# Attention and a gated feed-forward layer in one kernel: where v is loaded, and where the turned q and k are taken apart

## The chip, the core and the metric

The kernel runs on one core of a Trainium2 chip. The metric is device time in microseconds (us) for one execution. The core's engines run side by side, each on a queue of its own in a fixed order: TensorE (PE) for matmuls, VectorE (DVE), ScalarE (ACT), GpSimd (POOL), and SyncE (SP), which here only issues DMAs. ScalarE and GpSimd can issue DMAs too; such an issue stands in their queue between their other instructions. An engine that needs another's result waits at that instruction, and all behind it on the same engine waits with it.

## The reference

Eight batches of eight heads, 576 positions, head size 64. The scores get a bias from a running sum of `s`, a causal mask, a softmax, and are multiplied by v. The heads' outputs, laid side by side, are the 4608 x 512 input of a feed-forward layer with a hard-swish between its two products.

```python
scores = scale * np.matmul(q, k.transpose(0, 1, 3, 2))
cum = np.cumsum(np.maximum(s, 0.0), axis=-1)
bias = -(cum[:, :, :, None] - cum[:, :, None, :])
scores = np.where(causal, -1000000000.0, scores + np.minimum(bias, 0.0))
attn = softmax(scores)
x = np.matmul(attn, v)             # then to (4608, 512)
h = x @ w_in                       # 512 -> 2048
out = (h * np.clip(h + 3.0, 0.0, 6.0) / 6.0) @ w_out
```

## The kernel before

The 64 heads are worked in 32 pairs (two heads of one batch). Everything for TensorE is float16. For each pair q and k must stand with the head dimension on the partitions: `qT` and `kT`, two parts of `qkT`, in `NS` = 3 slots by pair number modulo 3. Rows 64 to 67 of a slot hold the bias terms (`load_aug`).

How q and k get there depends on the pair. Pairs 0 to 3 are cast and turned by TensorE (`cast_first`, `turn_first`, L825 to L837), pairs 4 to 9 as well (`transpose_group`, L301, L316). From pair `PTD` = 10 on, GpSimd casts them into `xb` (`cast_beside`, L282), SyncE issues a transposing DMA into `turned` (`transpose_dma`, L285), q in partitions 0 to 63 and k in 64 to 127, and VectorE copies both into the slot: `apart`, L293 for q and L294 for k.

v is loaded by `load_v` in three DMAs: one for each head's first 512 rows (L218) and one for the last 64 rows of both (L222). GpSimd casts it to `v_h` (`cast_v`, L298). v has three slots too.

`scores_bank` makes a head's scores in four pieces, each in one bank of PSUM (L350). ScalarE takes the exponential into `Pm` (L357), GpSimd zeroes what is above the diagonal (L362). The banks come from a ring of three (tag `S`), so a piece waits until the exponential three pieces earlier is done. `attend` multiplies with v (L447); VectorE divides by the row sums (L463, L464); `x_transpose` brings the result into `xT`, from pair 8 on by a transposing DMA on SyncE (L481).

The feed-forward layer goes in nine blocks of 512 rows. `m1` makes 128 of the 2048 columns (L526); ScalarE applies a relu with bias 3 (`trl`, L536), VectorE the gate (`gT`, L537), which frees the bank. `m2` is the second product (L569); its result goes through `osb` (L584) to the output (L586).

The order on each engine is the order of the calls in the program. Three stretches follow each other:

- a loop over the first eight heads (pairs 0 to 3). In it `cast_v(p)` is called at the first head of pair p. At pair 1 the two main loads of v of pair 3 are issued by GpSimd, its small one by SyncE. The weights are issued by GpSimd in and after this loop. A small DMA, the fence (L936), makes SyncE wait for `w_out`; the loads of later pairs stand behind it.
- pairs 4 to 8 in `second_pair`, among products of block 0.
- pairs 9 to 31 in `att_tasks`, which gives a list of small tasks with costs; `weave` deals them among the products of a block, in proportion to cost. For pair p the list has, in this order: `attend` of the earlier pair's second head, `x_transpose(p - 1)`, `loads` (q, k and v of pair p + 3), the four pieces of the first head (`s0`), those of the second (`s1`) with `apart(p + 1)` ahead of the third, `casts` (`cast_v(p + 1)`, `load_aug(p + 3)`, `cast_beside(p + 2)`, `transpose_dma(p + 2)`). `attend` of the first head follows.

Waits are on semaphores. The hardware DMAs share eight completion semaphores in turn, and a DMA first waits for the one before it on its semaphore.

Of the kernel before, what the change touches and what calls it, by code (L numbers as in the profile page):

```python
# [16 lines left out]
def kernel(  # L17
# [10 lines left out]
    nc = tc.nc  # L28
# [7 lines left out]
    W2 = 2 * SEQ  # L36
# [10 lines left out]
    PXD = 8  # L47
    NS = 3
# [37 lines left out]
    qT, kT = qkT[:, :, 0:W2], qkT[:, :, W2:SLOTW]  # L86
# [4 lines left out]
    turned = cpool.tile([128, 2, W2], F16, tag="c_turned")  # L91
# [106 lines left out]
    def qk_tile(p):  # L198
        qk_f[p] = work.tile([128, NTR, 2, D], F32, tag="qkf", bufs=3, name=f"qkf{p}")

    def load_part(p, i, t0, t1, eng):
        b, h0 = (2 * p) // H, (2 * p) % H
        rows = (q, k)[i][b, h0:h0 + 2].rearrange("h s d -> (h s) d")
        eng.dma_start(  # L204
            out=qk_f[p][:, t0:t1, i, :],
            in_=rows.rearrange("(t p) d -> p t d", p=128)[:, t0:t1, :],
        )

    def load_qk(p, eng):
        qk_tile(p)  # L210
        for i in range(2):
            load_part(p, i, 0, NTR, eng)

    def load_v(p, eng, main=None):
        b, h0 = (2 * p) // H, (2 * p) % H
        sl = p % NS
        for hh in range(2):
            (main or eng).dma_start(  # L218
                out=v_f[:, sl, hh, 0:4, :],
                in_=v[b, h0 + hh, 0:512].rearrange("(t p) d -> p t d", p=128),  # L220
            )
        eng.dma_start(  # L222
            out=v_f[0:64, sl, :, 4, :],
            in_=v[b, h0:h0 + 2, 512:SEQ].rearrange("h p d -> p h d"),
        )

    def load_aug(p, eng):
        sl = p % NS
        part = [h1 > 2 * p for _, h1 in PARTS].index(True)
        c0 = (2 * p - PARTS[part][0]) * SEQ  # L230
        eng.dma_start(
            out=qkT[64:68, sl, 0:2 * W2].rearrange("r (i c) -> r i c", i=2),
            in_=aug_dram[part][:, :, c0:c0 + W2].rearrange("i r c -> r i c"),
        )

    def cast_qk(p):
        t = work.tile([128, NTR, 2, D], F16, tag="qkh", bufs=2)
        src = qk_f.pop(p)
        for t0, t1 in ((0, 5), (5, 9)):
            nc.gpsimd.tensor_copy(out=t[:, t0:t1], in_=src[:, t0:t1])  # L240
        qk_h[p] = t
# [39 lines left out]
    def cast_beside(p):  # L281
        nc.gpsimd.tensor_copy(out=xb[:, p % 2], in_=qk_f.pop(p))  # L282

    def transpose_dma(p):
        nc.sync.dma_start(  # L285
            out=turned[:, p % 2, :].rearrange("p (t c) -> p t c", c=128),
            in_=xb[:, p % 2].rearrange("p t i d -> p (t i d)"),
            transpose=True,
        )

    def apart(p):
        sl = p % NS
        nc.vector.tensor_copy(out=qT[0:64, sl, :], in_=turned[0:64, p % 2, :])  # L293
        nc.vector.tensor_copy(out=kT[0:64, sl, 0:W2], in_=turned[64:128, p % 2, :])  # L294

    def cast_v(p):
        sl = p % NS
        nc.gpsimd.tensor_copy(out=v_h[:, sl, :, :, 0:D], in_=v_f[:, sl])  # L298
# [6 lines left out]
    def transpose_group(p, g):  # L305
        t0, t1 = ((0, 5), (5, 9))[g]
        n = (t1 - t0) * 128
        pT = f16(PS[:, 3, :], n)
        src = qk_h[p]
        for t in range(t0, t1):  # L310
            c = (t - t0) * 128
            transpose_tile(pT[:, c:c + 128], src[:, t, :, :], t == t0, t == t1 - 1)
        sl = p % NS
        c0 = t0 * 128
        for dst, r0 in ((qT, 0), (kT, 64)):
            nc.vector.tensor_copy(out=dst[0:64, sl, c0:c0 + n], in_=pT[r0:r0 + 64, 0:n])  # L316
        if g == 1:
            qk_h.pop(p)
# [152 lines left out]
    def by_dma(p):  # L471


        return PXD <= p < NP - 1

    def x_transpose(p):
        b, hp = p // (H // 2), p % (H // 2)
        xs = x_tiles.pop(p)
        if by_dma(p):

            nc.sync.dma_start(  # L481
                out=xT[:, hp, b * SEQ:b * SEQ + 640].rearrange("p (t c) -> p t c", c=128),
                in_=xs.rearrange("p t h d -> p (t h d)"),
                transpose=True,
            )
            return
        pX = f16(PS[:, 4 if p + 1 < FIRST else 2, :], 640) if p < FIRST else f16(bank("S"), 640)
        for qt in range(5):
            nc.tensor.matmul(
                out=pX[:, qt * 128:(qt + 1) * 128],  # L490
                lhsT=xs[:, qt, :, :],
                rhs=ident,
                is_transpose=True,
                start=(qt == 0),
                stop=(qt == 4),
            )
        nc.vector.tensor_copy(out=xT[:, hp, b * SEQ:(b + 1) * SEQ], in_=pX[:, 0:SEQ])
# [121 lines left out]
    def store_aug(part):  # L619
        h0, h1 = PARTS[part]  # L620
        nc.sync.dma_start(
            out=aug_dram[part].rearrange("i r (h t) -> h (i r) t", t=SEQ),
            in_=aug[h0:h1].rearrange("h i r t -> h (i r) t"),
        )

    def load_pair(p):
        load_qk(p, nc.sync)
        load_v(p, nc.sync)

    def scores(hd):  # L630
        return [(lambda bi=bi: scores_bank(hd, bi), 400) for bi in range(4)]
# [4 lines left out]
    def att_tasks(p):  # L636


        more = p + 1 < NP

        def loads():
            if p + 3 < NP:
                load_pair(p + 3)
            if p < PTD - 1:
                cast_qk(p + 1)

        def casts():
            if more:
                cast_v(p + 1)
            if p + 3 < NP:  # L650
                load_aug(p + 3, nc.sync)
            if p - PXD in (1, 2):
                store_aug(p - PXD + 2)
            if PTD <= p + 2 < NP:
                cast_beside(p + 2)
                transpose_dma(p + 2)

        tr = [[], []]
        if p + 1 < min(NP, PTD):
            tr = [[(lambda: transpose_group(p + 1, 0), 640)],  # L660
                  [(lambda: transpose_group(p + 1, 1), 512)]]
        late = [(lambda: attend(2 * p - 1), 600 if PTD <= p < PTD + 3 else 1200)]
        back = []
        if p > FIRST:
            back = [(lambda: x_transpose(p - 1), 0 if by_dma(p - 1) else 640)]
        a = [(loads, 0)]
        if p <= PXD:
            a += scores(2 * p) + tr[0] + late
            a += scores(2 * p + 1) + [(casts, 0)] + tr[1] + back
        else:  # L670
            s0, s1 = scores(2 * p), scores(2 * p + 1)
            a = late + (back + a if by_dma(p - 1) else a + s0[:2] + back)
            a += (s0 if by_dma(p - 1) else s0[2:]) + tr[0]
            if PTD <= p + 1 < NP:
                s1.insert(2, (lambda: apart(p + 1), 0))
            a += s1 + [(casts, 0)] + tr[1]
        return a, [(lambda: attend(2 * p), 1800 if PTD <= p + 1 < PTD + 3 else 1200)]

# [46 lines left out]
    def values(hd):  # L725
        return [
            [(lambda: attend(hd, range(0, 3)), 480)], [(lambda: attend(hd, range(3, 5)), 720)]
        ]

    att_of = [[]]  # L730
    for p in range(PXD, NP):
        a, c = att_tasks(p)
# [143 lines left out]
    def cast_pair(p):  # L876
        for i in range(2):
            cast_first(p, i, 0, NTR, G.tensor_copy)
            if p == 3 and i == 0:
                load_w_in(0)  # L880
        qk_f.pop(p)
# [3 lines left out]
    for hd in range(2 * FIRST):  # L885
        p, odd = hd // 2, hd % 2
        scores_half(hd, 0)
        if hd == 0:
            turn_first(0, 0, 5, 9, 6, V.tensor_copy)
            turn_first(0, 1, 5, 9, 5, V.tensor_copy)  # L890
        if not odd:
            if p == 0:
                cast_pair(1)
            if p == 2:
                load_w_in(1)
            cast_v(p)
            if p == 1:
                load_v(3, nc.sync, nc.gpsimd)
            if p + 1 < FIRST:
                turn_first(p + 1, 0, 0, 9, 4, V.tensor_copy)  # L900
            if p == 2:
                load_w_in(2)
            if p == 0:
                load_qk(3, nc.sync)
                nc.sync.dma_start(out=s_sb, in_=s.rearrange("b h t -> (b h) t"))
                load_v(2, nc.sync)
        elif p + 1 < FIRST:
            turn_first(p + 1, 1, 0, 9, 4, V.tensor_copy)
            if p + 2 < FIRST:
                cast_pair(p + 2)  # L910
        scores_half(hd, 1)
        if hd > 0:
            attend(hd - 1)
        if odd and p > 0:
            x_transpose(p - 1)
# [106 lines left out]
```

## Time and profile before

| what | value |
|---|---|
| median of 3 runs | 351.65 us (351.3 to 353.86) |
| profiled execution, and its span | 353.66 us, 351.9 us |
| granted TensorE clock | 1.000 |
| TensorE busy | 342.1 us, 97% of the span |
| VectorE, ScalarE, GpSimd busy | 58%, 59%, 42% |
| loads of v from SyncE, 128 KB each (L218) | 62, median 708 ns |
| loads of v from SyncE, 32 KB each (L222) | 32, median 627 ns |
| loads of v from GpSimd (L218) | 2, median 856 ns |

A line of the waits reads: engine, line, the engine and line it waited for, us in total, times, the longest. A line of the timeline reads: start, duration, engine, line, operation, what is written from what, and in brackets the idle time just before and what ended it. "SPq" is SyncE's issuing of a DMA: its duration is the issue, not the transfer. TensorE's matmuls overlap, so that its busy time is no measure of peak rate; gaps between its instructions are what counts here.

### The profile page before, as it was taken

To read this page: it belongs to the slowest core of one execution; us is meant where nothing else is said; L and a number is where in the kernel's file an instruction comes from. 1 tells how busy PE (TensorE), PEld (TensorE's weight loads), DVE (VectorE), ACT (ScalarE), POOL (GpSimd) and SP (SyncE) were. 2 spreads that over 40 slices of the span, in tenths; PEclk is the share of its full clock that TensorE was granted. 3 is DMA by queue.
4 is the path that set the end of the run, shared out by engine and by line. 5 is a ranking of instruction groups with operands and counts; after the bars stand their busy time and mean duration, and the time that the engine had idled before them with its cause. 6 is when DMAs were issued, how large, how long until landed. Compare 5 with 4: busy or idle time off the path is not lost.

```text
span 351.9 us, 7619 instructions
## 1 busy us (share of the span) xinstructions
PE 342.1 (97%) x2797; PEld 199.8 (57%) x2797; DVE 205.2 (58%) x375; ACT 208.7 (59%) x393; POOL 149.0 (42%) x322
## 2 busy tenths in 40 slices
PE   7899999999999899999999999999999999999996
PEld 3775457655555555555555555555555545444444
DVE  6559568887555783566546654756365635644531
ACT  4767747787655685677467755775577615534410
POOL 4685657744655356545435444454444200000000
PEclk9999999999999999999999999999999999999999
DMA  9999899999999888989898789788923110010012
GB/s 181 226 167 215 195 225 213 233 225 183 172 204 228 186 172 191 214 188 140 198 195 176 157 168 220 149 177 173 219 43 82 50 60 32 16 45 30 30 60 91
DMA packets 160271, 53.91 MB, mean 153 GB/s; under 512 B 152394, under 2 KB 154122, under 8 KB 160234
## 3 DMA queue, kind: packets, MB, share of 16 engines
q1 hardware_dynamic: 157178, 48.68, 63.9%
q0 software_dynamic: 2256, 4.46, 6.8%
q8 instruction: 22, 0.36, 0.4%
q10 hardware_dynamic: 800, 0.30, 0.3%
q14 instruction: 15, 0.12, 0.1%
HBM read 37.40 MB, written 9.95 MB: 135 GB/s over the span
## 4 chain that ended last, share of the span: by engine, by line
PE 76%; DMA 11%; DVE 4%; SPq 4%; POOL 2%; issue 1%; ACT 1%; POOLq 0%; ACTq 0%
PE PS L569 31%; PE PS L526 28%; PE PS L350 10%; PE PS L447 6%; DMA w_out_sb<-in_moe_w_out_dram 5%; DMA turned<-xb 3%; SPq L204 1%; SPq L218 1%; DMA qkf<-in_k_dram 1%; DVE gT L537 1%; DMA v_f<-in_v_dram 1%; DVE qkT L316 1%; PE PS L595 1%; DVE qkT L294 1%; PE PS L301 1%
## 5 line engine op out<-in xcount | busy, mean ns | idle before, releaser
L526 PE MATMUL PS<-xT,w_in 128*128 128x512 f16 x576 | 142.8, 380 | 1.8 <-DVE gT L537 1.8
L536 ACT ACTIVATE trl<-PS,bias 128x512 f32<-128x512 f32 x144 | 98.5, 693 | 74.3 <-PE PS L526 73.7
L537 DVE SCALAR_TENSOR_TENSOR gT<-trl,PS 128x512 f16<-128x512 f32 x144 | 97.4, 686 | 76.4 <-ACT trl L536 75.9
L569 PE MATMUL PS<-w_out_sb,gT 128*128 128x512 f16 x560 | 138.3, 379 | 0.0
L357 ACT ACTIVATE Pm<-PS 128x384 f16<-128x384 f32 x224 | 101.5, 508 | 41.6 <-PE PS L350 40.6
L362 POOL TENSOR_SCALAR_AFFINE_SELECT Pm<-Pm 128x64 f16<-128x64 f16 (+2 forms) x214 | 70.0, 330 | 111.3 <-ACT Pm L357 102.5
L526 PEld LDWEIGHTS <-w_in 128*128 128x128 f16 x576 | 60.3, 114 | 46.1 <-issue 2.4
L569 PEld LDWEIGHTS <-gT 128*128 128x128 f16 x560 | 51.1, 98 | 49.2 <-issue 0.3
L350 PE MATMUL PS<-qkT 128*128 128x256 f16 x392 | 61.5, 261 | 1.0 <-DVE qkT L294 0.6
L350 PEld LDWEIGHTS <-qkT 128*128 128x128 f16 x392 | 36.3, 98 | 30.3 <-DVE qkT L316 1.4
L447 PEld LDWEIGHTS <-Pm 128*128 128x128 f16 x960 | 38.0, 97 | 11.2 <-POOL Pm L362 0.3
L447 PE MATMUL PS<-v_h,Pm 128*128 128x65 f16 x960 | 41.1, 193 | 0.2 <-POOL Pm L362 0.2
L584 DVE TENSOR_SCALAR osb<-PS 128x512 f32<-128x512 f32 x34 | 23.4, 687 | 26.1 <-PE PS L569 26.1
L464 DVE TENSOR_TENSOR xs<-PS,r 128x640 f16<-128x640 f32 (+1 forms) x37 | 27.2, 735 | 1.3
L282 POOL CAST xb<-qkf 128x1152 f16<-128x1152 f32 x22 | 26.1, 1188 | 1.0 <-DMA qkf<-in_k_dram 1.0
L298 POOL CAST v_h<-v_f 128x640 f16<-128x640 f32 x32 | 23.7, 740 | 3.1 <-DMA v_f<-in_v_dram 3.0
L293 DVE COPY qkT<-turned 64x1152 f16<-64x1152 f16 x22 | 11.6, 527 | 11.5 <-DMA turned<-xb 11.5
L431 ACT ACTIVATE Pm<-PS 128x896 f16<-128x896 f32 (+1 forms) x16 | 13.1, 836 | 5.6 <-PE PS L425 5.5
L294 DVE COPY qkT<-turned 64x1152 f16<-64x1152 f16 x22 | 13.4, 611 | 0.3
L463 DVE RECIPROCAL r<-PS 128x10 f32<-128x10 f32 (+1 forms) x37 | 7.7, 209 | 6.1 <-PE PS L447 5.8
L316 DVE COPY qkT<-PS 64x640 f16<-64x640 f16 (+1 forms) x20 | 9.1, 454 | 2.3 <-PE PS L301 1.9
L425 PE MATMUL PS<-qkT 68*128 68x64 f16 (+4 forms) x48 | 9.1, 277 | 0.5 <-DVE qkT L837 0.4
(89 smaller groups left out, 115.4 us busy)
## 6 DMA issues: line engine op xcount, KB each, us to landing
out_dram<-osb SPq DMA_DIRECT2D x35, 256.0 KB, 2.6
qkf<-in_q_dram SPq DMA_DIRECT2D x31, 288.0 KB, 3.6
qkf<-in_k_dram SPq DMA_DIRECT2D x31, 288.0 KB, 4.1
v_f<-in_v_dram SPq DMA_DIRECT2D x62, 128.0 KB, 3.7
w_out_sb<-in_moe_w_out_dram POOLq DMA_DIRECT2D x4, 512.0 KB, 16.6
v_f<-in_v_dram SPq DMA_DIRECT2D x32, 32.0 KB, 2.6
w_in<-in_moe_w_in_dram POOLq DMA_DIRECT2D x2, 512.0 KB, 6.9
w_in<-in_moe_w_in_dram POOLq DMA_DIRECT2D x1, 1024.0 KB, 11.9
```

What stands on the lines that cost most here:

```text
L282: nc.gpsimd.tensor_copy(out=xb[:, p % 2], in_=qk_f.pop(p))
L298: nc.gpsimd.tensor_copy(out=v_h[:, sl, :, :, 0:D], in_=v_f[:, sl])
L350: nc.tensor.matmul(out=S[:, c:c + hi - lo], lhsT=kT[:, sl, off + 128 * kt:off + 128 * (kt + 1)], rhs=qT[:, sl, off + lo:off + hi], start=( ...
L357: nc.scalar.activation(out=P[:, p0:p0 + n], in_=S[:, 0:n], func=AF.Exp, scale=0.125, bias=0.0)
L362: nc.gpsimd.affine_select(out=view, in_=view, pattern=pattern, compare_op=ALU.is_ge, fill=0.0, base=0, channel_multiplier=-1,)
L447: nc.tensor.matmul(out=O[:, hh, qt * VW:qt * VW + D + 1], lhsT=P[:, c:c + 128], rhs=v_h[:, sl, hh, kt, 0:D + 1], start=(qt == 0), stop=(qt ...
L464: nc.vector.tensor_tensor(out=x_tiles[p].rearrange("p t h d -> p h t d")[:, heads], in0=Ov[:, :, :, 0:D], in1=r[:, 0:n].to_broadcast([128, ...
L526: nc.tensor.matmul(out=ph, lhsT=w_in_t[f // 4][:, kc, f % 4, :], rhs=xT[:, kc, n * 512:(n + 1) * 512], start=(kc == 0), stop=(kc == KC - 1),)
L536: nc.scalar.activation(out=trl, in_=ph, func=AF.Relu, bias=bias3[:, 0:1], scale=1.0)
L537: nc.vector.scalar_tensor_tensor(out=gT2[:, n % 2, f, :], in0=trl, scalar=6.0, in1=ph, op0=ALU.min, op1=ALU.mult)
L569: nc.tensor.matmul(out=po, lhsT=gT2[:, n % 2, f, t4 * 128:(t4 + 1) * 128], rhs=w_out_sb[:, f, :], start=(f == 0), stop=(f == NF - 1),)
L584: nc.vector.tensor_scalar_mul(out=osb, in0=pouts[n, t4], scalar1=1.0 / 6.0)
```

## The change

It has three parts.

1. In the loop over the first pairs, `load_v(3, ...)` is called ahead of `cast_v(1)`, where it was called behind it. On GpSimd the two issues now stand ahead of the cast; SyncE's part stands where it stood.
2. `apart` copies one of q and k. For pairs 10 to 31 the copy of q stays where it was, ahead of the third piece of the second head; the copy of k comes behind the fourth piece.
3. In pairs 11, 12 and 13 (`V_BY_ACT`) v of pairs 14, 15 and 16 is no longer issued by SyncE behind q and k, but by ScalarE behind the fourth piece of the first head: three DMAs each time.

```diff
-    def apart(p):
-        sl = p % NS
-        nc.vector.tensor_copy(out=qT[0:64, sl, :], in_=turned[0:64, p % 2, :])
-        nc.vector.tensor_copy(out=kT[0:64, sl, 0:W2], in_=turned[64:128, p % 2, :])
+    def apart(p, i):
+        nc.vector.tensor_copy(
+            out=(qT, kT)[i][0:64, p % NS, 0:W2], in_=turned[64 * i:64 * i + 64, p % 2, :]
+        )
...
             if p + 3 < NP:
-                load_pair(p + 3)
+                load_qk(p + 3, nc.sync)
+                if p not in V_BY_ACT:
+                    load_v(p + 3, nc.sync)
...
             a += (s0 if by_dma(p - 1) else s0[2:]) + tr[0]
+            if p in V_BY_ACT:
+                a.append((lambda: load_v(p + 3, nc.scalar), 0))
             if PTD <= p + 1 < NP:
-                s1.insert(2, (lambda: apart(p + 1), 0))
+                s1.insert(2, (lambda: apart(p + 1, 0), 0))
+                s1.append((lambda: apart(p + 1, 1), 0))
             a += s1 + [(casts, 0)] + tr[1]
...
+    V_BY_ACT = range(PXD + 3, PXD + 6)
     att_of = [[]]
...
                 load_w_in(1)
-            cast_v(p)
             if p == 1:
                 load_v(3, nc.sync, nc.gpsimd)
+            cast_v(p)
```

## The prediction

> **What bounds the kernel now.** I read the page's busy shares first, then who waited for whom, then stretches of the timeline around each wait of TensorE.
>
> ```profile
> PE 342.1 (97%) x2797; PEld 199.8 (57%) x2797; DVE 205.2 (58%) x375; ACT 208.7 (59%) x393; POOL 149.0 (42%) x322
> PE PS L526 <- DVE gT L537: 1.8, 2, 1.3
> PE PS L831 <- POOL gT L825: 1.3, 2, 0.9
> PE PS L350 <- DVE qkT L294: 0.6, 1, 0.6
> DVE qkT L293 <- DMA turned<-xb: 11.5, 9, 4.0
> ```
>
> TensorE is busy 97%, and its list of waits is short: less than 10 us idle in 352, and from 118 us to 345 us it is never idle. A change can win only these idles, and loses whenever it makes a new one, because a late TensorE catches up nowhere. Three idles touch the edited lines. The first is at 17 us:
>
> ```profile
> 14.15 0.72 POOL L298 CAST v_h<-v_f 128x640 f16<-128x640 f32 x1 [1.59 <-DMA v_f<-in_v_dram]
> 14.82 1.70 POOL L218 DMA_DIRECT2D v_f<-in_v_dram  x2
> 16.50 0.69 POOL L825 CAST gT<-qkf 128x576 f16<-128x576 f32 x1
> 17.25 0.69 PE L831 MATMUL PS<-idtri,gT 128*68 128x128 f16 x9 [0.90 <-POOL gT L825]
> ```
>
> GpSimd waits 1.59 us for v of pair 1, casts it, and only then spends 1.70 us issuing v of pair 3; the cast that TensorE needs stands behind. The others lie where pairs 12 and 14 are prepared:
>
> ```profile
> 94.43 1.65 SPq L285 DMA_TRANSPOSE turned<-xb  x1
> 98.65 0.98 DVE L293 COPY qkT<-turned 64x1152 f16<-64x1152 f16 x1 [3.99 <-DMA turned<-xb]
> 99.65 1.30 DVE L294 COPY qkT<-turned 64x1152 f16<-64x1152 f16 x1
> 101.01 0.34 PE L350 MATMUL PS<-qkT 128*128 128x256 f16 x2 [0.61 <-DVE qkT L294]
> 114.89 0.55 DVE L293 COPY qkT<-turned 64x1152 f16<-64x1152 f16 x1 [0.78 <-DMA turned<-xb]
> 115.45 1.31 DVE L294 COPY qkT<-turned 64x1152 f16<-64x1152 f16 x1
> 116.79 1.88 DVE L537 SCALAR_TENSOR_TENSOR gT<-trl,PS 128x512 f16<-128x512 f32 x3
> 117.53 1.89 PE L526 MATMUL PS<-xT,w_in 128*128 128x512 f16 x8 [1.26 <-DVE gT L537]
> 99.76 1.71 SPq L218 DMA_DIRECT2D v_f<-in_v_dram  x2
> 101.51 0.63 SPq L222 DMA_DIRECT2D v_f<-in_v_dram  x1
> ```
>
> The two copies wait for the transposed load, which is late because SyncE issues without a gap from 40.05 us (the fence behind w_out) to 127 us; v takes 1.71 + 0.63 = 2.34 us of each pair's issuing. In time of issue TensorE loses about 0.75 us at 101 us, 1.4 us at 117.5 us, and a third idle at 82.4 us (0.6 us, gT behind the two copies of pair 10).
>
> **What the Trainium skill says.** Perfetto Trace Analysis, "What 'DMA-bound' means": an issuing sequencer whose track is solid DMA slices is itself a bound. The trace agrees for SyncE, 40 to 127 us. The same page, "DMA Instruction — HWDGE (DVE, Sync)": the sequencer is held for the lock on a shared descriptor generator and while it works, and is free only at the reported end. The trace agrees for SyncE (slices 0.04 to 0.1 us apart); it has no such load amid ScalarE's exponentials. DMA: Bandwidth & Descriptors, "Issuing engines are not separate DMA queues": another issuer saves the sequencer's time, not transfer time; no line of before tests it. SBUF — State Buffer, "SBUF: two separate sides": VectorE's fast modes and GpSimd exclude each other for a whole instruction. The trace agrees: the k copy takes 0.46 us, and 1.30 us where it meets GpSimd's 1.38 us cast at 99.27 us.
>
> **The change part by part.**
>
> *v of pair 3 ahead of the cast.* The two issues keep their price (1.70 us) but fall into GpSimd's 1.59 us of waiting, which starts at 12.56: done at 14.26, the cast until 14.98, then q of pair 3, whose load I place at about 15.2 (issued at 10.93; the two before it took some 4 us). That cast ends near 15.9, before TensorE asks at 16.24. TensorE gains 1.0 us. The gain lasts only if SyncE's chain moves too, since TensorE meets it at 101 us. That chain begins when w_out lands (40.04 us); the weights stream at a DMA share above 1 from 20 us, after a dip to 0.51 at 18 to 19 us, and their first load is issued about 1.0 us earlier. So **−1.0 us**, between −1.2 and 0 (0 if the early bytes only delay v of pair 1 or w_out).
>
> *Copies apart.* 22 more places in the order, no new work. Pair 9: one gT product moves ahead of the 0.46 us k copy, **−0.46 us**. In pairs 10 to 12 the two copies stay neighbours on VectorE. From pair 14 on the k copy comes up to about 1 us later; what hides it is the two attends and the products between the last score of a pair and the next pair's first (144.28 us against a k copy done at 141.33). It now falls nearer to GpSimd's casts and may take 1.3 instead of 0.46 us; gT waits 76 us for ScalarE in all, so that is room: 0, with +1.5 us as the other bound.
>
> *v of pairs 14 to 16 by ScalarE.* Nine issues leave SyncE (3 x 2.34 us). In the built program every hardware DMA first waits for the one eight places back on the shared completion semaphores, whichever engine issues it: transposes of x on SyncE now stand behind a v that ScalarE has to issue (pair 10's behind v of pair 14: issued about 96.1, landing near 99, so it goes 2 us later than its 97.20). The slot's earlier cast is long done. So SyncE gains little for pair 13's load, and two to three us for pair 14's, which GpSimd's cast then sets.
> On ScalarE the three issues hold back four exponentials of the second head. The score ring has three banks, so the second head's fourth score waits for its first exponential. The price on ScalarE is unknown: 1.4 us with the shortest v issue of SyncE (0.379 twice, 0.6), 2.34 us at SyncE's usual, 3 us if each also waits for SyncE's turn. I take 2.0 us, 0.4 of it under the exponential ahead, which is still running: 1.6 us. Then:
> - pair 11: the first exponential ends at about 96.5, the fourth score starts at 97.5: slack 0.95, stall 0.65 us. It meets the 0.75 us idle at 101 us and the 0.46 us of pair 9, 1.2 us together: **−0.55 us for both**. The k copy can follow it, since GpSimd's cast is late as well and no longer meets it.
> - pair 12: slack 0.25 us, and a 0.16 us gap ahead of pair 13 goes: 1.6 − 0.25 − 0.16 = **+1.2 us**.
> - pair 13: behind a relu of 0.69 us that hides part of it, no slack: +1.3 us. The 1.4 us idle at 117.5 goes, since copy and gT are no longer late against TensorE; the k copy now sits between two gT products and costs about 0.4 us: **+0.3 us**.
>
> Sum: −1.0 − 0.55 + 1.2 + 0.3 = −0.05 us. To this I add 0.4 us for transfers that now run beside pair 12's transposed load (4.19 us already) and for longer k copies: **+0.35 us**. The profiled execution took 353.66 us (span 351.9 and 1.8 around it), so it would take 354.0. It stands 2.0 us above the median of the runs shown, 351.65; the forecast for the median is **352.0 us**.
>
> **The rivals.**
> 1. ScalarE's issues are nearly hidden (0.8 us left). For it: 0.47 us for its only early load, and an empty ring of its own. Pair 11 costs nothing and wins 1.2, pair 12 costs 0.4, pair 13 wins 0.9: −1.0 − 1.2 + 0.4 − 0.9 = −2.7, 349.0 us. Against it: v takes SyncE 1.5 to 1.9 us for two even at 212 to 251 us, where the transfers are less dense.
> 2. Slower: ScalarE's issues stand in SyncE's way and are stood in the way of, at pairs 11 to 13, 1 us each, 3 us a pair. Pair 11 +0.45, pair 12 +2.2, pair 13 +1.3, and nothing won at the start: +3.95, 355.6 us. It passes +1% (3.5 us) from about 0.95 us an issue, if the start wins nothing. For it: SyncE is solid there. Against it: 0.71 us is the median of a v issue.
> 3. The early order gives nothing (SyncE's chain, held by bandwidth, takes it back at 101 us) and the rest is as forecast: 353.0 us.
>
> **How the numbers follow.** Forecast 0.55 (350.8 to 353.4), rival 1 0.20, rival 2 0.13, rival 3 0.12. Leaving out the lower half of rival 1 and the upper of rival 2 gives 349.8 to 354.9. About 1% (3.5 us) is what a measurement of this kernel tells from no change: faster by more needs nearly all idle gone, 0.03; slower by more is rival 2's upper part and what I overlook, 0.11; within, 0.86.
>
> **What would show it.** Right: no wait of L831 for GpSimd at 16 us, w_out landing near 39 us, new idles of TensorE at L350 <- ScalarE L357 in pairs 12 and 13 of 1 to 1.5 us, no idle for gT after pair 13, ScalarE's v issues of 0.5 to 0.8 us each. Wrong: those issues below 0.4 us or above 1 us, a wait of ScalarE for a DMA, or new idles after 125 us from late k copies.

## The result, and the profile after

| | before | after |
|---|---|---|
| median of 6 runs | 352.33 us (351.30 to 353.86) | 355.76 us (355.26 to 357.67) |
| ratio, with 95% interval | | 1.0092 (1.0066 to 1.0118) |
| profiled execution, and its span | 353.66 us, 351.9 us | 355.26 us, 353.5 us |

The kernel became slower by 0.9%, some 3.2 us. The forecast was no change, 352.0 us in a range to 354.9; it was wrong. The two profiled executions differ by only 1.6 us: that of before stands 1.3 us above its median, that of after 0.5 us below. The traces show where time goes; how much it is in the mean, the ratios of many runs tell.

TensorE's share of after, and who waited for whom:

```profile
PE 342.6 (97%) x2797; PEld 200.2 (57%) x2797; DVE 207.7 (59%) x375; ACT 209.1 (59%) x393; POOL 149.1 (42%) x322
PE PS L350 <- ACT Pm L357: 3.6, 4, 1.5
PE PS L526 <- DVE gT L537: 0.4, 1, 0.4
PE PS L837 <- POOL gT L831: 0.4, 1, 0.4
DVE qkT L292 <- DMA turned<-xb: 12.7, 5, 4.7
```

TensorE does the same work. Its waits for gT at L526 went from 1.8 to 0.4 us. Those for GpSimd's casts of q and k went from 1.3 to 0.4 us: the one at 17 us (0.9 us) is gone, an earlier one of 0.4 us stays. The wait for a k copy is gone too. One new wait outweighs them: scores that wait for ScalarE's exponential.

The start of after, timeline of GpSimd:

```profile
12.38 1.70 POOL L218 DMA_DIRECT2D v_f<-in_v_dram  x2
14.06 0.74 POOL L298 CAST v_h<-v_f 128x640 f16<-128x640 f32 x1
15.37 0.67 POOL L831 CAST gT<-qkf 128x576 f16<-128x576 f32 x1 [0.56 <-DMA qkf<-in_q_dram]
18.84 0.72 POOL L298 CAST v_h<-v_f 128x640 f16<-128x640 f32 x1 [0.76 <-DMA v_f<-in_v_dram]
```

This is as forecast: the issues lie in the former wait, and the cast of q of pair 3 starts at 15.37 instead of 16.50. Further back GpSimd waits 0.76 us for v of pair 2, where it had not waited.

Pair 11 of after, ScalarE ("ACTq" is its issuing of a DMA), and TensorE at the fourth scores of the second heads of pairs 11, 12 and 13:

```profile
93.97 0.49 ACT L357 ACTIVATE Pm<-PS 128x384 f16<-128x384 f32 x1 [0.27 <-PE PS L350]
94.20 0.38 ACTq L218 DMA_DIRECT2D v_f<-in_v_dram  x1
94.35 0.43 ACT L357 ACTIVATE Pm<-PS 128x320 f16<-128x320 f32 x1
94.68 1.19 ACTq L218 DMA_DIRECT2D v_f<-in_v_dram  x1
95.96 0.69 ACTq L222 DMA_DIRECT2D v_f<-in_v_dram  x1
96.75 1.69 ACT L357 ACTIVATE Pm<-PS 128x384 f16<-128x384 f32 x4 [1.97 <-PE PS L569]
97.30 0.30 PE L350 MATMUL PS<-qkT 128*128 128x320 f16 x1 [1.01 <-ACT Pm L357]
105.50 0.30 PE L350 MATMUL PS<-qkT 128*128 128x320 f16 x1 [1.45 <-ACT Pm L357]
114.39 0.30 PE L350 MATMUL PS<-qkT 128*128 128x320 f16 x1 [0.96 <-ACT Pm L357]
```

The first exponential of the second head waits behind the issues, and the score that needs its bank waits with it. Where TensorE stands at the first score of each pair:

| first score of pair | before | after | difference |
|---|---|---|---|
| 11 | 93.64 | 92.29 | −1.35 |
| 12 | 101.01 | 100.07 | −0.94 |
| 13 | 108.64 | 109.43 | +0.79 |
| 14 | 119.25 | 120.35 | +1.10 |
| 16 | 135.95 | 137.54 | +1.59 |

TensorE of after is ahead by 1.35 us when it comes to pair 11, loses 2.45 us until pair 14 and 0.5 us until pair 16. From there the difference stays.

### The profile page after: what moved, and what is told of

The parts are those of the page before. It is cut to its first block, busy times and chain, and to the rows that moved or that the text cites. A ratio compares the mean times of both kernels' runs of the same rounds, so it can differ in the third digit from the quotient of the medians.

```text
span 353.5 us, 7655 instructions
## 1 busy us (share of the span) xinstructions
PE 342.6 (97%) x2797; PEld 200.2 (57%) x2797; DVE 207.7 (59%) x375; ACT 209.1 (59%) x393; POOL 149.1 (42%) x322
## 4 chain that ended last, share of the span: by engine, by line
PE 82%; SPq 4%; ACT 3%; DVE 3%; DMA 3%; issue 2%; POOL 2%; ACTq 1%; POOLq 0%
PE PS L569 32%; PE PS L526 31%; PE PS L350 9%; PE PS L447 7%; DMA turned<-xb 2%; ACT Pm L357 2%; SPq L204 1%; SPq L218 1%; DVE gT L537 1%; DVE qkT L292 1%; DMA v_f<-in_v_dram 1%; PE PS L595 1%; ACT trl L536 1%; POOL Pm L362 1%; PE PS L301 1%
## 5 line engine op out<-in xcount | busy, mean ns | idle before, releaser
L526 PE MATMUL PS<-xT,w_in 128*128 128x512 f16 x576 | 142.7, 379 | 0.5 <-DVE gT L537 0.4
L357 ACT ACTIVATE Pm<-PS 128x384 f16<-128x384 f32 x224 | 101.6, 509 | 45.1 <-PE PS L350 40.7
L362 POOL TENSOR_SCALAR_AFFINE_SELECT Pm<-Pm 128x64 f16<-128x64 f16 (+2 forms) x214 | 69.2, 326 | 116.3 <-ACT Pm L357 107.3
L526 PEld LDWEIGHTS <-w_in 128*128 128x128 f16 x576 | 60.2, 113 | 45.7 <-issue 1.9
L350 PE MATMUL PS<-qkT 128*128 128x256 f16 x392 | 61.8, 261 | 4.0 <-ACT Pm L357 3.6
L350 PEld LDWEIGHTS <-qkT 128*128 128x128 f16 x392 | 36.3, 98 | 29.7 <-DVE qkT L316 1.4
L292 DVE COPY qkT<-turned 64x1152 f16<-64x1152 f16 x44 | 28.6, 650 | 13.3 <-DMA turned<-xb 12.7
```

The costliest lines, as they stand in the source:

```text
L292: nc.vector.tensor_copy(out=(qT, kT)[i][0:64, p % NS, 0:W2], in_=turned[64 * i:64 * i + 64, p % 2, :])
L350: nc.tensor.matmul(out=S[:, c:c + hi - lo], lhsT=kT[:, sl, off + 128 * kt:off + 128 * (kt + 1)], rhs=qT[:, sl, off + lo:off + hi], start=( ...
L357: nc.scalar.activation(out=P[:, p0:p0 + n], in_=S[:, 0:n], func=AF.Exp, scale=0.125, bias=0.0)
L362: nc.gpsimd.affine_select(out=view, in_=view, pattern=pattern, compare_op=ALU.is_ge, fill=0.0, base=0, channel_multiplier=-1,)
L526: nc.tensor.matmul(out=ph, lhsT=w_in_t[f // 4][:, kc, f % 4, :], rhs=xT[:, kc, n * 512:(n + 1) * 512], start=(kc == 0), stop=(kc == KC - 1),)
```

## The experiments

Two theories at first. A: ScalarE's issues hold the second head's exponentials, and that is the whole loss. B: the k copies behind the fourth piece make it. Later C: SyncE's waits for transfers that ScalarE issues.

### Each part alone

Only the loads by ScalarE (SyncE no longer issues them, as in the change):

```diff
+            if p in V_BY_ACT:
+                a.append((lambda: load_v(p + 3, nc.scalar), 0))
```

> Only the loads of v of pairs 14 to 16 go to ScalarE; order of v of pair 3 and the copies as before. Theory A (ScalarE's issues hold the second head's exponentials, and that is the whole loss): idles of TensorE at L350 behind ScalarE of 1.0, 1.5 and 1.0 us in pairs 11 to 13, and +3 to +4 us against before, as much as the whole change or a little more. Theory B (the k copies behind the fourth piece make the loss): the loads alone cost under 1 us, since the idles of before at 101 and 117 us take them up.

Measured: 1.0072 (1.0045 to 1.0099), 2.5 us, with 1.6 to 3.5 us in the interval. B, which gave this part under 1 us, falls by this ratio; the part alone is most of the loss. For A it is a little less than expected.

Its profiled execution is a poor sample. From 84 to 90 us the granted TensorE clock was 0.50 to 0.85, and by 92 us TensorE was 3.4 us behind the trace of before, although ScalarE's first load is issued only at 98.97 us. From 92 us on the clock is 1.00, and the three idles are there:

```profile
101.41 0.30 PE L350 MATMUL PS<-qkT 128*128 128x320 f16 x1 [0.36 <-ACT Pm L357]
109.34 0.30 PE L350 MATMUL PS<-qkT 128*128 128x320 f16 x1 [1.17 <-ACT Pm L357]
118.07 0.30 PE L350 MATMUL PS<-qkT 128*128 128x320 f16 x1 [1.11 <-ACT Pm L357]
```

But from there to the end it loses only 0.75 us more against the trace of before, because the idles that before had at 101 and 117.5 us are gone, as B had it. The ratio speaks for more; why this one trace shows less stays open.

Only the copies apart (`apart` takes one of the two, as in the change):

```diff
-                s1.insert(2, (lambda: apart(p + 1), 0))
+                s1.insert(2, (lambda: apart(p + 1, 0), 0))
+                s1.append((lambda: apart(p + 1, 1), 0))
```

> Only the copies of q and k apart. Theory A: within 0.5 us of before, no idle of TensorE for a copy. Theory B: +2 us or more, with idles at L526 or L569 behind gT where a k copy stands between two products of the gate, one or two of them after 125 us.

Measured: 1.0013 (0.9998 to 1.0028). Set matmul by matmul against before, each counted from its first, TensorE wins 0.72 us at 78 to 84 us and gives 0.64 us back between 122 and 135 us. The give-back is in all eight profiles with the copies apart (0.48 to 0.64 us) and in none of the four others that have them together (0.00 us). Its place, with the k copy of pair 15 in before (first line) and then VectorE and the product behind it in after:

```profile
125.00 0.46 DVE L294 COPY qkT<-turned 64x1152 f16<-64x1152 f16 x1
128.04 1.10 DVE L292 COPY qkT<-turned 64x1152 f16<-64x1152 f16 x1
129.17 0.69 DVE L537 SCALAR_TENSOR_TENSOR gT<-trl,PS 128x512 f16<-128x512 f32 x1
130.77 1.87 DVE L537 SCALAR_TENSOR_TENSOR gT<-trl,PS 128x512 f16<-128x512 f32 x3
131.50 1.02 PE L569 MATMUL PS<-w_out_sb,gT 128*128 128x512 f16 x4 [0.18 <-DVE gT L537]
```

In after the k copy runs beside GpSimd's cast (127.68 to 128.83 us), takes 1.10 us for 0.46, and the gate's products behind it are late for the first product of `m2`. It is not the only one: of the 44 copies of q and k, 38 to 42 took under 0.6 us in the five profiles with the copies together, 25 to 31 in the eight with them apart.

Only v of pair 3 early:

```diff
-            cast_v(p)
             if p == 1:
                 load_v(3, nc.sync, nc.gpsimd)
+            cast_v(p)
```

> Only v of pair 3 asked for ahead of the cast. Both theories: the wait of L831 for GpSimd at 17 us is gone, w_out lands 2 to 3 us earlier. If TensorE keeps that, -1.0 us; if it is given back at the transposed loads of pairs 12 and 14, within 0.3 us of before.

Measured: 0.9999 (0.9984 to 1.0013), so between −0.6 and +0.5 us. The wait at 17 us is gone, and w_out landed at 38.95 us, 1.1 us earlier, less than expected. But in this execution 0.69 us is won by 16.5 us and only 0.15 us is left at 20.5 us. The first line is before, the others are this run:

```profile
19.18 0.77 POOL L298 CAST v_h<-v_f 128x640 f16<-128x640 f32 x1
19.31 0.72 POOL L298 CAST v_h<-v_f 128x640 f16<-128x640 f32 x1 [0.98 <-DMA v_f<-in_v_dram]
20.08 0.58 PE L447 MATMUL PS<-v_h,Pm 128*128 128x65 f16 x14 [0.48 <-POOL v_h L298]
```

GpSimd comes to the cast of v of pair 2 earlier than in before, but v of pair 2 is not there earlier. So GpSimd waits 0.98 us for it, and TensorE 0.48 us for GpSimd. All nine profiles with the early order show such a wait of GpSimd, of 0.7 to 1.0 us. The cast begins at 18.7 to 19.7 us in them, and at 19.1 to 19.7 us in the four with the old order; that the early bytes made v of pair 2 later is not shown.

How much TensorE keeps differs from one execution to the next. At 40 us, matmul by matmul against before, it stands at −0.8 to +0.3 us in the nine (mean −0.3) and at −0.1 to +0.5 us in the four, before among them (mean +0.1). Nor was the idle at 17 us in each: in the run with only ScalarE's loads, which has the old order, GpSimd waited 0.53 us for v of pair 1 and not 1.59, and the idle is not there. It then waited 0.89 us for v of pair 2 all the same.

The kernel before, once more:

> The kernel before, looked at once more, since its six runs lie in two groups (351.3 to 351.7 and 353.0 to 353.9) and its profiled run is in the upper. If the groups differ by the idles at 101 and 117 us, a run near 351.5 shows less than 1 us of idle for L294 and gT there, and the gain that the forecast saw in them is mostly not there. If they do not, its trace has both idles (0.6 and 1.3 us) as the first has. Time: 1.000 of before.

Measured: 1.0015 (0.9997 to 1.0033); the profiled execution took 353.75 us. TensorE's waits for gT, and for a copy of k:

```profile
PE PS L526 <- DVE gT L537: 1.9, 2, 1.5
PE PS L350 <- DVE qkT L294: 0.2, 1, 0.2
```

The idle for gT is there, that at 101 us is not. So the idle at 101 us comes and goes from one execution to the next. What an execution of 351.3 us looks like stays open; none was profiled.

### The hold of ScalarE by itself

The changed kernel again, then without these loads:

> The changed kernel once more, beside the others of this call. Ratio to before 1.006 to 1.012, and again three idles of TensorE for ScalarE at L350 in pairs 11 to 13, 3 to 4 us in all.

Measured: 1.0076 (1.0048 to 1.0105), waits at L350 for ScalarE of 3.9 us.

```diff
-            if p in V_BY_ACT:
-                a.append((lambda: load_v(p + 3, nc.scalar), 0))
```

> The changed kernel without any load of v of pairs 14 to 16 (the slots keep older values, so the output of these pairs is not the reference's). ScalarE is not held and SyncE is relieved. Theory A (the hold of ScalarE is the loss): no idle at L350 for ScalarE, 3 to 4.5 us under the changed kernel, so 0.5 to 1 us under before. Theory C (SyncE's waits for transfers of another engine's issue are the loss): about as theory A. If it stays over +0.5% against before, neither holds, and the loss lies in the copies.

Measured: 0.9954 (0.9935 to 0.9972). No score waits for ScalarE beyond 0.2 us. SyncE issues pair 14's transposed load at 106.95 us, against 111.18 in before. So SyncE's relief is worth something, 0.4% against the two other parts without it (0.9996, measured below), and ScalarE's three times three issues take it back three times over. This run lacks the transfers of these v as well as their issues; the run with the same loads behind the second head (0.9947, below) has them and is as fast, so the gain is not that of missing transfers.

ScalarE held without any DMA (`scratch` is a tile for this alone):

```diff
+    def hold():
+        for _ in range(4):
+            nc.scalar.copy(out=scratch, in_=warm)
...
-                a.append((lambda: load_v(p + 3, nc.scalar), 0))
+                a.append((hold, 0))
```

> As the run without loads of v of pairs 14 to 16, but with four copies of 128 x 512 in fp16 on ScalarE where the three issues stood, some 2.0 to 2.3 us of work without any DMA (the output of these pairs is not the reference's). Theory A: as slow as the changed kernel within 1 us, with the same three idles at L350. Theory C: as fast as the run without the loads.

Its lines are numbered one higher: L351 is L350 of before, L358 is L357. ScalarE's copies, and TensorE:

```profile
96.14 2.57 ACT L639 COPY scratch<-warm 128x512 f16<-128x512 f16 x4
104.93 2.56 ACT L639 COPY scratch<-warm 128x512 f16<-128x512 f16 x4
114.76 2.56 ACT L639 COPY scratch<-warm 128x512 f16<-128x512 f16 x4
99.15 0.30 PE L351 MATMUL PS<-qkT 128*128 128x320 f16 x1 [1.40 <-ACT Pm L358]
107.93 0.30 PE L351 MATMUL PS<-qkT 128*128 128x320 f16 x1 [2.02 <-ACT Pm L358]
117.75 0.30 PE L351 MATMUL PS<-qkT 128*128 128x320 f16 x1 [2.21 <-ACT Pm L358]
```

Measured: 1.0141 (1.0111 to 1.0171). The stand-in is longer than meant, 2.56 us, and the three idles grow with it, to 5.6 us. The time was expected within 1 us of the changed kernel and is 2.3 us over. The longer idles make 1.9 us in the traces (scores for ScalarE: 5.8 us for 3.9). But three of the six executions also had a mean clock of 0.994 to 0.995, which none of the changed kernel's six had, and the other three are only 1.2 us over; how the excess divides is not settled. C falls as the explanation: the loss is there without a transfer.

### The same loads in other places

Behind the second head, where ScalarE then has nothing to do for 2.4 us in pair 11 and 3.4 us in pair 12:

```diff
-            if p in V_BY_ACT:
-                a.append((lambda: load_v(p + 3, nc.scalar), 0))
...
+            if p in V_BY_ACT:
+                s1.append((lambda: load_v(p + 3, nc.scalar), 0))
```

> The changed kernel with ScalarE's loads moved behind the fourth piece of the second head, where ScalarE stands idle for about 3 us in pairs 11 and 12; in pair 13 four relus stand behind them. Theory A: no idle at L350 for ScalarE, pairs 11 and 12 cost nothing, pair 13 costs up to 1.5 us at L526 behind gT; in all 0.995 to 1.004 of before. Theory C: still slow, 1.006 or more, since the loads land later still and SyncE waits longer for them.

ScalarE of this kernel in pair 11, and all waits of TensorE between 90 and 136 us:

```profile
97.06 0.44 ACT L357 ACTIVATE Pm<-PS 128x320 f16<-128x320 f32 x1 [0.19 <-PE PS L350]
97.16 1.08 ACTq L218 DMA_DIRECT2D v_f<-in_v_dram  x2
98.34 0.69 ACTq L222 DMA_DIRECT2D v_f<-in_v_dram  x1
99.86 0.49 ACT L357 ACTIVATE Pm<-PS 128x384 f16<-128x384 f32 x1 [2.37 <-PE PS L350]
107.30 0.56 PE L350 MATMUL PS<-qkT 128*128 128x256 f16 x4 [0.24 <-DVE qkT L292]
116.20 1.02 PE L526 MATMUL PS<-xT,w_in 128*128 128x512 f16 x4 [0.40 <-DVE gT L537]
128.21 1.02 PE L569 MATMUL PS<-w_out_sb,gT 128*128 128x512 f16 x4 [0.18 <-DVE gT L537]
```

Measured: 0.9947 (0.9930 to 0.9964), 351.76 us: under both kernels, with the same loads by the same engine. The nine issues last nearly as long as in after (4.9 us for 5.3 us), and the next exponential, the first of pair 12, waits for its scores, not for them. This settles A against C.

One exponential later than in after:

```diff
-            if p in V_BY_ACT:
-                a.append((lambda: load_v(p + 3, nc.scalar), 0))
...
+            if p in V_BY_ACT:
+                s1.insert(1, (lambda: load_v(p + 3, nc.scalar), 0))
```

> The changed kernel with ScalarE's loads one exponential later: behind the first piece of the second head in place of behind the last of the first. Theory A as the ring of three banks has it: the fourth piece of the second head needs only the first piece's exponential, which now stands ahead of the loads, so the idles at L350 for ScalarE are gone, 0.995 to 1.001 of before. If any hold of ScalarE among the scores costs its length, the time stays at 1.006 or more.

Measured: 1.0052 (1.0036 to 1.0067). The idles at L350 for ScalarE are gone, so the ring of three banks is how the hold reached the scores. But most of the loss is still there, against what was expected. VectorE and TensorE of this kernel:

```profile
99.89 1.86 DVE L292 COPY qkT<-turned 64x1152 f16<-64x1152 f16 x2 [5.45 <-DMA turned<-xb]
117.63 1.27 DVE L292 COPY qkT<-turned 64x1152 f16<-64x1152 f16 x1
101.81 0.34 PE L350 MATMUL PS<-qkT 128*128 128x256 f16 x2 [2.06 <-DVE qkT L292]
116.37 1.02 PE L526 MATMUL PS<-xT,w_in 128*128 128x512 f16 x4 [0.49 <-DVE gT L537]
119.67 1.02 PE L526 MATMUL PS<-xT,w_in 128*128 128x512 f16 x4 [0.96 <-DVE gT L537]
```

Two other waits have come. Pair 12's transposed load is issued at 94.93 us and done only at 99.89, after 5.0 us. In the run with the loads behind the second head it was issued 1.3 us earlier and took 3.3 us (93.62 to 96.95), with v of pair 14 issued after it was done; here v was issued beside it, from 94.99 us. That it is issued later is not v's doing, since ScalarE's first issue comes after it. In pair 13 a relu now stands behind the issues and its gT comes late (0.49 us at 116.37). The 0.96 us at 119.67 stands behind the long k copy, as 0.44 us does at that place in after.

Whether v made the load slow was not tried by itself, but the other profiles point to it. From its issue to VectorE's first copy this load took 4.70, 4.73 and 4.96 us in the three profiles where ScalarE issued v of pair 14 within 1 us of it (after, after again, this one), and 3.30 to 4.22 us in the ten others.

### The other two parts without ScalarE's loads, and the best place without the copies apart

> The changed kernel without ScalarE's loads: v of pair 3 early and the copies apart, all v from SyncE. Theory A, from the parts measured alone (0.9999 and 1.0013): 0.999 to 1.002 of before, so nothing of the loss is in these two parts, nor in their meeting. If they do bad together, 1.004 or more.

Measured, all v from SyncE again: 0.9996 (0.9979 to 1.0013). So the two parts and their meeting show no loss beyond this interval (−0.7 to +0.5 us). In its trace the idle at 117.5 us is gone too, with 0.40 us left behind the k copy of pair 14: not all of that idle hangs on SyncE's relief.

The kernel with the loads behind the second head, with `apart` as before:

> The kernel with ScalarE's loads behind the second head, but with both copies together as before (v of pair 3 early). If the copies apart earn nothing once ScalarE is out of the way: 0.993 to 0.998 of before, like the run with them apart (0.9947). If they earn the 0.46 us at 82 us for good: 0.5 to 1 us slower than that run.

Measured: 0.9975 (0.9960 to 0.9990). The intervals of this and of the run with the copies apart (0.9930 to 0.9964) overlap by a hair (0.9960 to 0.9964), and they were measured in two sessions on two chips. Its trace has no give-back between 122 and 135 us and a span of 349.8 us against 350.3. Whether the copies apart pay is not settled.

## Why the prediction was wrong

The mechanism and its place were named: the hold, the three banks, the fourth score, and three new idles at L350. The sum around it was wrong, above all on the side of the gains. In the two profiled executions, by the steps of the forecast (idles as time of issue):

| step | forecast | in the traces |
|---|---|---|
| v of pair 3 early | −1.0 | −0.62 |
| pair 9, a gT product ahead of k | −0.46 | −0.74 |
| pair 11, stall | +0.65 | +1.19 |
| idle at 101 us goes | −0.75 | −0.75 |
| pair 12, stall | +1.35 | +1.61 |
| gap ahead of pair 13 | −0.16 | +0.11 |
| pair 13, stall | +1.3 | +1.12 |
| idle at 117.5 us goes | −1.4 | −1.4 |
| gT behind the k copy, pair 13 | +0.4 | +0.6 |
| later | +0.4 | +0.5 |
| sum | +0.35 | +1.6 |

**The hold** was about right: 2.0 us for three issues forecast, 2.26 us in pair 11 and some 1.6 us of issuing in 12 and 13 measured. What was missed in pair 11 is one issue of 1.19 us that ran while SyncE issued a store (95.00, 0.98 us). In pair 12 the third issue starts 0.54 us after the second has ended, held by the landing of q of pair 14 (the trace names it as what ended ScalarE's wait). The prediction followed such semaphore waits for SyncE and left them out for ScalarE. The three stalls come to 3.9 us for 3.3.

**The gains failed.** The ratios give them without the luck of one execution. Forecast: −1.0 for v of pair 3, −0.46 for the copies, and about −2.2 for idles that SyncE's relief removes. Measured: 0.9999 for the first, 1.0013 for the second, 0.9996 for both, so no gain beyond 0.2%. SyncE's relief with ScalarE left alone is worth 0.9954 against 0.9996, some 1.5 us from two sessions. From 0.9954 the issues in their place bring it to 1.0076 and 1.0092, a loss of 4.3 to 4.9 us. So about −1.5 us of gain stood where I had put −3.7, and this is the larger error. The step that failed for v of pair 3 is "the gain lasts only if SyncE's chain moves too": the chain did move (w_out landed at 37.4 us for 40.0), but v of pair 2 came no earlier, and GpSimd and TensorE waited for it. I had not followed that cast. At 40 us, 0.4 us is left in the mean of the profiles where I had put 1.0, and the ratio shows none. For the copies it is "what hides it is the two attends": true for the scores, but the longer copy (1.10 us for 0.46) holds the gate's products, which I had priced at 0 with +1.5 us as the bound.

**The anchor.** I set the forecast 2.0 us under the sum because before's profiled run stood that far above the median of three. The six runs of the result have a median of 352.33. In later runs beside the experiments before lay at 353.0 to 353.8 us, and its second profiled run has the same span within 0.1 us but not the idle at 101 us. An idle of one profiled execution was counted as if each had it.

**A reading.** SyncE's issues from 40 to 127 us were called without a gap; one gap of 0.45 us lies at 63.4 us. Nothing in the sum rests on it.

**The rivals.** The nearest is rival 2, 355.6 us with a chance of 0.13, and that it comes so near is in part luck. It was right that the start wins nothing, but its issues of 1 us each were not there: the nine took 0.37 to 1.19 us, 0.6 us in the mean. Rival 3 was right on the start's worth, not on where it is lost: in the trace of the run with that part alone most of it is handed back at 20 us, before SyncE's chain comes into it.

**The range** left out the upper part of rival 2, the one case in which long stalls and a missing gain at the start come together. That is where the measured time lies.

## What to carry to other kernels

Here a DMA issue on a compute engine was an instruction of some 0.4 to 1.2 us in its queue. Put it where that engine waits for others anyway, and count every instruction behind it up to the next buffer that someone needs. The same nine issues cost 4.3 us or more ahead of the second head's exponentials and nothing measurable behind them, a few places later. What the transfer runs beside may count too: one exponential later the scores no longer stood, but TensorE waited for a transposed load beside which v had been issued. That v slowed this load is likely, not shown. And an idle in one profiled execution is a gain only if it is there in others; a second look at the kernel before costs less than a wrong sum.

## What the runs showed of the hardware that I had not expected

- ScalarE's 36 issues of 128 KB of v in six runs took 0.37 to 1.22 us, with a median of 0.45 us against 0.59 us on SyncE in the same runs. Its 18 of 32 KB took 0.61 to 1.11 us, with a median of 0.69 us against 0.63 us. So a queue with no other DMA in it made the large ones a little cheaper and the small ones not.
- An issue can begin before the exponential that stands ahead of it in ScalarE's order: in pair 11 the first began at 94.20 us, that exponential (128 x 320) at 94.35 us.
- A copy of 64 x 1152 in fp16 on VectorE takes 0.46 us alone and 1.1 to 1.3 us beside a cast on GpSimd, so moving it by two scores changed its price more than its place.
- With v of pair 3 (256 KB) issued some 2 us earlier, w_out landed at 37.4 to 39.1 us in nine profiles, for 39.0 to 40.5 us in the four with the old order. The ranges meet, so a single pair of profiles would not have shown it.
